# Long convolution and spectral mixing on one NeuronCore: the first tick of a pair moved to PSUM banks 6 and 7, in two parts by channels

## The chip, the cores and the metric

The kernel runs on one core of a Trainium2 chip. The metric is the device time of one execution in microseconds (us). The engines are TensorE (PE in the profile, its weight loads PEld), VectorE (DVE), ScalarE (ACT), GpSimd (POOL) and SyncE (SP); the last two mostly issue DMAs here.

## The reference

The input x has 8 batches of 5696 positions and 128 channels; h has one filter a channel. The first step is a causal convolution along the positions, the second a mixing of the 64 lowest modes with a relu layer behind it:

```python
def _attn_ref(x, h):                      # x: (8, 5696, 128), h: (5696, 128)
    L = 2 * S
    Yf = np.fft.rfft(x, n=L, axis=1) * np.fft.rfft(h, n=L, axis=0)[None]
    return np.fft.irfft(Yf, n=L, axis=1)[:, :S, :]

def _moe_ref(x, w_r, w_i, w_ch):          # x: what _attn_ref gave
    X = np.fft.rfft(x, axis=1)
    Y[:, :64] = X[:, :64] mixed over channels by the complex w_r + i w_i, per mode
    u = x + np.fft.irfft(Y, n=S, axis=1)
    return u + np.maximum(u @ w_ch, 0.0)
```

## The kernel before

The 5696 positions are 89 rows (`NQ`) of 64 columns (`J`). The batches go in four pairs (`NP`, index `g_`; the two batches of a pair are `b` = 0 and 1). The Fourier transform of a pair is done in two steps of matmuls:

1. **First transform, 32 tiles** (`a_tile`, L461). Tile j has four matmuls of 180 columns (input `Xin`, constant `F`) into two PSUM banks, for the channels 4j to 4j+3. VectorE or ScalarE copies the result into `As` in SBUF; tile 31 is copied half by each ("both"). Tiles 6 to 31 of the next pair are made between two pairs, in the loop at L740: this is the *border*. Tile 28 lies in banks 6 and 7, tile 29 in 0 and 1, tile 30 in 2 and 3, tile 31 in 4 and 5. The copies of 28 and 30 are ScalarE's, that of 29 VectorE's.
2. **23 ticks** (`tick`, L649; `NT` = 23, four frequencies of 90 each). Tick t has
   - the *second transform* (`second`, L605): for each of four frequencies and two parts (`r`) a pair of matmuls, one for each batch, on 64 rows of the array each (`As` with the constant `M`, 64x128). The result for batch 0 goes to one bank, that for batch 1 to the next one (`slot_of`, L600). A matmul takes all 128 channels, so it needs the copies of all 32 tiles;
   - the *products* with the filter's spectrum `Hs` on VectorE into `U` (`products`, L616). In most ticks ScalarE first copies both banks to `Xs` (SBUF), and VectorE reads that (L637). In tick 0, VectorE takes batch 0 straight from PSUM, while ScalarE copies batch 1's bank to `Xs`, from which VectorE then takes it (L629). Every fourth tick (t % 4 == 3, pairs 1 to 3) reads PSUM straight for both.
   - two ticks later (`LC`): four matmuls with 512 columns of `U` (constant `Wc`) into one of the banks 4, 5, 6 (`ZBANK`) for each batch, copied by ScalarE to `Zs`, and written to HBM by a DMA on SP's queue;
   - three ticks later (`LM`): matmuls of `Zs` with `G` that add up in bank 7 (`MB`).

In the first pair (`g_` = 0), the ticks up to 16 also make the filter's spectrum (`filter_tick`, L486: matmuls `Ah` with `M` into banks 2 and 3, copied to `Hs` by VectorE), and all second transforms of these ticks use banks 0 and 1. In the later pairs, odd ticks from 1 on do the second transform of the next tick as well (`twin`).

Order of work: every engine runs its instructions in the order in which the program adds them. A recorder (L22) keeps, for each token (a bank, an `As` tile, a `U` buffer), its last writer and readers, and puts semaphore waits ahead of an instruction from them. Matmuls do not wait for matmuls; two VectorE instructions that write the same `U` token do wait for each other. An instruction that waits holds all those behind it on its engine.

At a border the order on TensorE is: tile 31, eight dummy matmuls into banks 6 and 7 (`keep(8, 6)`, L743; they use only the constant `F` and nobody reads them), tick 0's second transform into banks 0 and 1, tick 1's into banks 2 and 3, tick 2's into banks 0 and 1, then tick 0's four `U` matmuls.

After the four pairs comes a last stage (from `mix`, L806): mixing of the modes (`XT` with `W`), the inverse transform (`ZT`, `S4`, `IBs`, `C`) and the relu layer (`WI`), with DMAs of the output.

Of the kernel before, what the change touches and what calls it, by code (L numbers as in the profile page):

```python
# [4 lines left out]
P = 128  # L5
# [118 lines left out]
def bass_long_conv_fft__then__afno_spectral_mix_kernel(nc, x, h, moe_w_r, moe_w_i, moe_w_ch, out):  # L124
    B, S, D = x.shape
# [159 lines left out]
    def ap(t, row, p0, n, off, dims):  # L285
        return bass.AP(t, p0 * row + off, [[row, n]] + [list(d) for d in dims])
# [5 lines left out]
    def pv(bank, off, dims, p0=0, n=P):  # L292
        return bass.AP(ps, p0 * 4096 + bank * 512 + off, [[4096, n]] + [list(d) for d in dims])
# [28 lines left out]
    def mm(o, l, r, st, sp, reads, writes):  # L322
        R.add("tensor", lambda h_: h_.matmul(o, l, r, start=st, stop=sp), reads, writes)  # L323
# [100 lines left out]

    W1, W2, WI = wc_sb[:, 0:P], wc_sb[:, P:2 * P], wi_sb[:, :]
    XSLOT = [0, 2]
    ZBANK = [4, 5, 6]
    MB = 7
    WARM = 92
# [152 lines left out]
    def with_h_at(g_, t):  # L582
        return g_ == 0 and t + LH < NT
# [14 lines left out]
        return g_ > 0 and t % 4 == 3  # L598

    def slot_of(g_, t):  # L600
        if g_ == 0 or t == 0:
            return XSLOT[(t + 1) % 2 if t and not with_h_at(g_, t) else 0]
        return XSLOT[((t - 1) // 4 + t) % 2]

    def second(g_, t):  # L605
        sl = slot_of(g_, t)
        for i, k in enumerate(ticks[t]):
            for r in range(2):
                for b in range(2):
                    col = k * 3 * J + (J if r == 0 else 0) + b * J  # L610
                    mm(pv(sl + b, i * D, [[1, D]]),
                       ap(m_sb, MW, J * b, J, col, [[1, P]]),
                       ap(a_sb, AW, J * b, J, (2 * k + r) * D, [[1, D]]), r == 0, r == 1,
                       AST + mtok(k), [bank(sl + b)])

    def products(g_, t, sl):  # L616
        n = len(ticks[t])
        bk = [bank(sl), bank(sl + 1)]
        i = t % NU
        hv = bass.AP(h_sb, KT * t * D, [[2 * HW, P], [HW, 2], [0, 2], [1, n * D]])  # L620
        uv = bass.AP(u_s[i], 0, [[2048, P], [1024, 2], [512, 2], [1, n * D]])
        src = pv(sl, 0, [[0, 2], [512, 2], [1, n * D]])
        if t == 0:
            e = turns("e", list(range(NXS)))
            evac(bass.AP(x_s[e], 512, [[1024, P], [1, n * D]]), pv(sl + 1, 0, [[1, n * D]]), [bank(sl + 1)], [("xs", e)], eng="scalar")
            hv = bass.AP(h_sb, 0, [[2 * HW, P], [HW, 2], [1, n * D]])
            for b, s_, tok in ((0, pv(sl, 0, [[0, 2], [1, n * D]]), bank(sl)),
                               (1, bass.AP(x_s[e], 512, [[1024, P], [0, 2], [1, n * D]]), ("xs", e))):
                R.add("vector", lambda e, b=b, s_=s_: e.tensor_tensor(bass.AP(u_s[i], b * 512, [[2048, P], [1024, 2], [1, n * D]]), s_, hv, MULT),  # L629
                      [tok, ("h", t, 0), ("h", t, 1, 0), ("h", t, 1, J)], [("u", i)])  # L630
            return
        if not straight(g_, t):
            e = onchip.get((g_, t))
            if e is None:
                e = copied(g_, t, sl)
            src, bk = bass.AP(x_s[e], 0, [[1024, P], [0, 2], [512, 2], [1, n * D]]), [("xs", e)]
        R.add("vector", lambda e: e.tensor_tensor(uv, src, hv, MULT),  # L637
              bk + [("h", t, 0), ("h", t, 1, 0), ("h", t, 1, J)], [("u", i)])
# [10 lines left out]
    def tick(g_, t):  # L649
        if g_ + 1 < NP:  # L650
            for i in range(2 * XC):
                if t == XPLACE[g_ > 0][i]:
                    x_place(i, bass.AP(x_room(g_ + 1, i), 0, [[XB, NQ], [D, XN], [1, D]]), xtok(i))
        with_h = with_h_at(g_, t)
        if t < NT:
            of_two = t > 0 and twin(g_, t - 1)
            if not of_two:
                second(g_, t)
            products(g_, t, slot_of(g_, t))
            if twin(g_, t):  # L660
                second(g_, t + 1)
                if straight(g_, t):
                    copied(g_, t + 1, slot_of(g_, t + 1))
        drain = list(border[t]) if t in border and g_ + 1 < NP else []
        if drain and t >= NT:
            j, sl, e = drain.pop(0)
            a_tile(j, [sl], e)
        if g_ + 1 < NP:
            i = t // 2 - 1 if t % 2 == 0 else -1
            if g_ == 0:  # L670
                i = XLATE.index(t) + NXH if t in XLATE else -1
            if 0 <= i < 2 * XC:
                x_load(g_ + 1, i, x_room(g_ + 1, i), xtok(i), [("u", t % NU)] + AST)
        if LC <= t < NT + LC:
            s_ = t - LC
            n = len(ticks[s_])
            i, zi = s_ % NU, zroom(g_, s_)
            zb = [turns("z", ZBANK) for b in range(2)]
            for b in range(2):
                for r in range(2):  # L680
                    mm(pv(zb[b], 0, [[1, n * D]]), (W1, W2)[r], u_s[i][:, r * 1024 + b * 512:r * 1024 + b * 512 + n * D],
                       r == 0, r == 1, [("u", i), ("wc",)], [bank(zb[b])])
                evac(bass.AP(z_s[zi], b * D, [[1024, P], [2 * D, n], [1, D]]),
                     pv(zb[b], 0, [[D, n], [1, D]]), [bank(zb[b])], [("zs", zi, b)], eng="scalar",
                     after=once(("zx", zi, b), Z_OLD) if zi >= NZ else ())
            zo = (g_ * NK + KT * s_) * P * 256
            dma("sync", bass.AP(zs, zo, [[256, P], [P * 256, n], [1, 256]]),
                bass.AP(z_s[zi], 0, [[1024, P], [256, n], [1, 256]]), "z",
                [("zs", zi, 0), ("zs", zi, 1)], [("zd", g_, s_)])
            if drain and t >= NT:  # L690
                j, sl, e = drain.pop(0)
                a_tile(j, [sl], e)
        if LM <= t < NT + LM:
            s_ = t - LM
            zi = zroom(g_, s_)
            for i, k in sorted(enumerate(ticks[s_]), key=lambda q: (s_ > 0 or q[1] != 1, q)):
                for b in range(2):
                    if k % 2:
                        o, off, n, sl = pv(MB, b * P, [[1, P]]), (k + 1) // 2 * P, P, (k + 1) // 2
                    else:  # L700
                        ms, off = even[k]
                        n, sl = 2 * len(ms), 0
                        dims = [[M, 2]] if len(ms) == 1 else [[ms[1] - ms[0], 2], [M, 2]]
                        o = pv(MB, b * P + ms[0], dims)
                    mm(o, z_s[zi][:, i * 256 + b * P:i * 256 + b * P + P], g_sb[:, off:off + n],
                       k == 1 and b == 0, k == NK - 1 and b == 1, [("g", sl // GP), ("zs", zi, b)], [bank(MB)])
        if drain and t < NT + LM - 1:
            j, sl, e = drain.pop(0)
            a_tile(j, [sl], e)
        if with_h:  # L710
            filter_tick(t + LH, [2, 3])
# [11 lines left out]
    for g_ in range(NP):  # L723
        if g_ == NP - 1:
            load_w(0)
            load_w(1)
        for t in range(NT + LM):
            tick(g_, t)
            if g_ == 0 and t < 2:
                keep(8, 4)  # L730
            assert g_ + 1 < NP or not wp
            if g_ == NP - 1 and t in early:
                pace[:] = [("u", min(t, NT - 1) % NU)]
                early[t]()
        evac(bass.AP(xt, 2 * g_ * XTW + M, [[B * XTW, P], [XTW, 2], [1, P]]), pv(MB, 0, [[P, 2], [1, P]]),
             [bank(MB)], [("xt", g_)], 1.0 / 64, eng="scalar", after=[("ag", k) for k in range(NS + 2 * XN, NK)])
        evac(bass.AP(xt, 2 * g_ * XTW, [[B * XTW, P], [XTW, 2], [1, M]]), pv(MB, M, [[P, 2], [1, M]]),
             [bank(MB)], [("xtn", g_)], -1.0 / 64, eng="vector" if g_ + 1 == NP else "scalar", after=[("ag", k) for k in range(NS + 2 * XN, NK)])
        if g_ + 1 < NP:
            for j in range(6, 32):  # L740
                a_tile(j, [(4, 6, 0, 2)[(j - 7) % 4] if j > 6 else 0], "both" if j == 31 else (A, V)[(j - 6) % 9 % 2])
                if j == 31:
                    keep(8, 6)  # L743
                if wp and j % 2 == 1:
                    dst, src_, ring, tok = wp.pop(0)
                    dma("gpsimd", dst, src_, ring, (), [tok], after=[("as", j)])
# [192 lines left out]
```

## Time and profile before

| what | us |
|---|---|
| median of 3 runs | 382.4 (381.59 to 383.15) |
| the profiled execution | 381.7 |
| its span, first to last instruction | 379.9 |
| TensorE busy | 359.7 |
| ScalarE busy | 314.4 |
| VectorE busy | 294.9 |
| GpSimd busy | 75.1 |

The mean clock granted to TensorE was 0.989 of full speed. The three borders lie at about 90 to 107, 146 to 162 and 201 to 217 us of the span; the last stage begins at about 258 us.

How to read the profile: a row of the timeline has the start and length in us, the engine, the line of the program, the operation, the output and input by name and shape, how many instructions were merged into the row, and in brackets how long the engine stood idle before and what ended that. The chain of waits is the sequence of work and waits that ended last, followed back from the last instruction; each piece has its start and length. A group row has busy time and the mean length of one in ns. Matmuls overlap: one of 128 columns shows 0.22 us, though the next pair starts 0.06 us later.

### The profile page before, as it was taken

To read this page: it belongs to the slowest core of one execution; us is meant where nothing else is said; L and a number is where in the kernel's file an instruction comes from. 1 tells how busy PE (TensorE), PEld (TensorE's weight loads), DVE (VectorE), ACT (ScalarE), POOL (GpSimd) and SP (SyncE) were. 2 spreads that over 40 slices of the span, in tenths; PEclk is the share of its full clock that TensorE was granted. 3 is DMA by queue.
4 is the path that set the end of the run, shared out by engine and by line. 5 is a ranking of instruction groups with operands and counts; after the bars stand their busy time and mean duration, and the time that the engine had idled before them with its cause. 6 is when DMAs were issued, how large, how long until landed. Compare 5 with 4: busy or idle time off the path is not lost.

```text
span 379.9 us, 12434 instructions
## 1 busy us (share of the span) xinstructions
PE 359.7 (95%) x5346; PEld 278.9 (73%) x5346; DVE 294.9 (78%) x333; ACT 314.4 (83%) x495; POOL 75.1 (20%) x117
## 2 busy tenths in 40 slices
PE   7889899999989999989999999999999999999994
PEld 7778766666856666856667856668889889988873
DVE  3649799878988999989998888882437767766666
ACT  8469689898989997989997999995457776788884
POOL 8713012100642220733310301124000000000000
PEclk9999999999999999999999999998899999999999
DMA  7999959979799997999995989999999999999878
GB/s 149 206 292 362 248 147 231 236 205 267 87 143 202 238 250 217 103 125 212 259 253 168 95 302 364 372 360 383 372 390 376 374 412 404 418 405 382 319 296 320
DMA packets 87048, 103.94 MB, mean 274 GB/s; under 512 B 22730, under 2 KB 72522, under 8 KB 83438
## 3 DMA queue, kind: packets, MB, share of 16 engines
q1 hardware_dynamic: 64610, 81.33, 60.7%
q0 software_dynamic: 22384, 21.83, 34.8%
q8 instruction: 42, 0.69, 0.7%
q14 instruction: 12, 0.10, 0.1%
HBM read 70.61 MB, written 51.12 MB: 320 GB/s over the span
## 4 chain that ended last, share of the span: by engine, by line
PE 66%; ACT 13%; DVE 7%; DMA 6%; issue 4%; POOL 3%; DVEq 0%; ACTq 0%; POOLq 0%
PE ps L323 65%; ACT As L313 7%; DMA Xr<-in_x_dram 4%; DVE As L317 2%; ACT Zs L311 2%; DMA zscr<-Zs 2%; DVE U L629 2%; ACT Zt L311 2%; POOL Xr L320 2%; ACT Xs L311 1%; DVE Xin L365 1%; ACT R L871 1%; POOL Hin L320 1%; DVE U L637 1%; DVE Hs L315 1%
## 5 line engine op out<-in xcount | busy, mean ns | idle before, releaser
L637 DVE TENSOR_TENSOR U<-Xs,Hs 128x2048 f16<-128x2048 f16 (+1 forms) x73 | 86.9, 1192 | 14.3 <-ACT Xs L311 11.3
L323 PE MATMUL ps<-U,Wc 128*128 128x512 f16 (+1 forms) x368 | 94.2, 376 | 0.5 <-DVE U L629 0.5
L311 ACT CAST Xs<-ps 128x1024 f16<-128x1024 f32 (+1 forms) x77 | 75.0, 978 | 12.3 <-PE ps L323 7.3
L311 ACT CAST Zs<-ps 128x512 f16<-128x512 f32 (+1 forms) x132 | 69.2, 594 | 2.0 <-PE ps L323 1.7
L872 DVE TENSOR_TENSOR O<-ps,R 128x512 f32<-128x512 f32 x81 | 52.3, 684 | 20.1 <-ACT R L871 11.2
L317 DVE TENSOR_SCALAR As<-ps 128x720 f16<-128x720 f32 (+1 forms) x67 | 55.6, 880 | 5.7 <-PE ps L323 4.0
L871 ACT ACTIVATE R<-ps 128x512 f32<-128x512 f32 (+1 forms) x92 | 50.5, 591 | 8.5 <-PE ps L323 8.4
L323 PE MATMUL ps<-F,Xin 128*128 128x180 f16 x512 | 52.4, 250 | 3.7 <-DVE Xin L365 2.2
L323 PE MATMUL ps<-As,M 64*128 64x128 f16 x1440 | 50.3, 217 | 3.8 <-DVE U L629 3.0
L323 PEld LDWEIGHTS ps<-F,Xin 128*128 128x128 f16 x512 | 44.5, 155 | 11.1 <-DVE As L317 3.2
L313 ACT ACTIVATE As<-ps 128x720 f16<-128x720 f32 (+1 forms) x65 | 45.8, 768 | 7.2 <-PE ps L323 6.6
L323 PE MATMUL ps<-WI,UT 128*128 128x256 f16 x360 | 51.1, 278 | 0.5 <-ACT UT L311 0.4
L311 ACT CAST UT<-ps 128x712 f16<-128x712 f32 x46 | 34.5, 752 | 19.2 <-PE ps L323 18.0
L323 PEld LDWEIGHTS ps<-U,Wc 128*128 128x128 f16 x368 | 28.6, 97 | 29.7 <-ACT Zs L311 3.8
L323 PEld LDWEIGHTS ps<-As,M 64*128 64x128 f16 x1440 | 40.5, 94 | 10.0 <-DVE U L629 3.7
L323 PEld LDWEIGHTS ps<-WI,UT 128*128 128x128 f16 x360 | 39.0, 152 | 3.4 <-issue 1.8
L323 PE MATMUL ps<-IBs,C 128*128 128x356 f16 x128 | 40.3, 325 | 0.1
L320 POOL DMA_DIRECT2D Xt<-in_x_dram x40 | 21.5, 541 | 81.2 <-PE ps L323 80.7
L323 PEld LDWEIGHTS ps<-G,Zs 128*128 128x128 f16 x512 | 26.1, 96 | 14.5 <-ACT Zs L311 2.0
L637 DVE TENSOR_TENSOR U<-ps,Hs 128x2048 f16<-128x2048 f32 x15 | 34.3, 2284 | 0.0
L323 PE MATMUL ps<-G,Zs 128*128 128x128 f16 (+2 forms) x512 | 32.2, 192 | 0.1
L311 ACT CAST Zt<-ps 128x512 f16<-128x512 f32 x52 | 28.5, 622 | 0.2 <-PE ps L323 0.2
(74 smaller groups left out, 489.0 us busy)
## 6 DMA issues: line engine op xcount, KB each, us to landing
out_dram<-O SPq DMA_DIRECT2D x39, 512.0 KB, 6.9
zscr<-Zs SPq DMA_DIRECT2D x62, 256.0 KB, 6.8
zscr<-Zt SPq DMA_DIRECT2D x26, 256.0 KB, 6.7
Xt<-in_x_dram POOLq DMA_DIRECT2D x20, 320.0 KB, 7.3
W<-wscr SPq DMA_DIRECT2D x4, 1024.0 KB, 7.0
ZT0a<-zscr SPq DMA_DIRECT2D x4, 1024.0 KB, 8.2
M<-cM POOLq DMA_DIRECT2D x5, 720.0 KB, 17.0
ZT1a<-zscr SPq DMA_DIRECT2D x3, 1024.0 KB, 8.3
```

Source lines behind the costliest of these rows:

```text
L311: R.add(e, lambda h_: h_.copy(dst, src), reads, writes, after=after)
L313: R.add(e, lambda h_: h_.activation(dst, src, COPY, scale=scale), reads, writes, after=after)
L315: R.add(e, lambda h_: h_.tensor_copy(dst, src), reads, writes, after=after)
L317: R.add(e, lambda h_: h_.tensor_scalar_mul(dst, src, scale), reads, writes, after=after)
L320: R.add(eng, lambda h_: h_.dma_start(dst, src), reads, writes, ring=ring, after=after)
L323: R.add("tensor", lambda h_: h_.matmul(o, l, r, start=st, stop=sp), reads, writes)
L365: R.add("vector", lambda e: e.tensor_copy(bass.AP(x_sb, i * XN * XS, [[XW, NQ], [XS, XN], [1, D]]), src), list(toks) + XZ, [("xin", i)])
L629: R.add("vector", lambda e, b=b, s_=s_: e.tensor_tensor(bass.AP(u_s[i], b * 512, [[2048, P], [1024, 2], [1, n * D]]), s_, hv, MULT), [tok, ...
L637: R.add("vector", lambda e: e.tensor_tensor(uv, src, hv, MULT), bk + [("h", t, 0), ("h", t, 1, 0), ("h", t, 1, J)], [("u", i)])
L871: R.add("scalar", lambda e: e.activation(rv, src_r, RELU), bk, [("r", i % NR)], after=once(("r", i % NR), G_ALL + XTT + [("y", 0), ("y", 1 ...
L872: R.add("vector", lambda e: e.tensor_tensor(ov, src_u, rv, ADD), bk + [("r", i % NR)], [key + (h_,)], after=once(key, old))
```

## The change

Tick 0's second transform uses banks 6 and 7 (`ZSLOT`) in every pair. For the pairs 1 to 3 it is cut by channels (`DA` = 116): the channels 0 to 115, which come from the tiles 0 to 28, take the place of the dummies, behind tile 31's matmuls, and wait for the copies of the tiles 0 to 28 only. In tick 0, batch 0's product for these channels is taken from PSUM; then come the last 12 channels of batch 1 (bank 7), ScalarE's copy of bank 7 and batch 1's product. The last 12 channels of batch 0 (bank 6) come in tick 1, behind tick 1's second transform, with a third, small product.

```diff
+    ZSLOT, DA = 6, 116
     def slot_of(g_, t):
-        if g_ == 0 or t == 0:
-            return XSLOT[(t + 1) % 2 if t and not with_h_at(g_, t) else 0]
+        if t == 0:
+            return ZSLOT
+        if g_ == 0:
+            return XSLOT[(t + 1) % 2 if not with_h_at(g_, t) else 0]
         return XSLOT[((t - 1) // 4 + t) % 2]
-    def second(g_, t):
+    def second(g_, t, d0=0, d1=D, bs=(0, 1)):
         sl = slot_of(g_, t)
+        rd = AST if d1 == D else [("as", j) for j in range(d1 // 4)]
         for i, k in enumerate(ticks[t]):
             for r in range(2):
-                for b in range(2):
+                for b in bs:
...
-                    mm(pv(sl + b, i * D, [[1, D]]),
+                    mm(pv(sl + b, i * D + d0, [[1, d1 - d0]]),
...
+    def first_u(b, s_, row, tok, d0, d1):
+        n = len(ticks[0])
+        R.add("vector", lambda e: e.tensor_tensor(
+            bass.AP(u_s[0], b * 512 + d0, [[2048, P], [1024, 2], [D, n], [1, d1 - d0]]),
+            bass.AP(s_[0], s_[1] + d0, [[row, P], [0, 2], [D, n], [1, d1 - d0]]),
+            bass.AP(h_sb, d0, [[2 * HW, P], [HW, 2], [D, n], [1, d1 - d0]]), MULT),
+              [tok, ("h", 0, 0), ("h", 0, 1, 0), ("h", 0, 1, J)], [("u", 0)])
     def products(g_, t, sl):
...
+            if g_ == 0:
+                copy_b()
+                first_u(0, (ps, sl * 512), 4096, bank(sl), 0, D)
+                first_u(1, (x_s[e], 512), 1024, ("xs", e), 0, D)
+                return
+            first_u(0, (ps, sl * 512), 4096, bank(sl), 0, DA)
+            second(g_, 0, DA, D, (1,))
+            copy_b()
+            first_u(1, (x_s[e], 512), 1024, ("xs", e), 0, D)
             return
...
             if not of_two:
-                second(g_, t)
+                if g_ == 0 or t:
+                    second(g_, t)
+                if g_ and t == 1:
+                    second(g_, 0, DA, D, (0,))
+                    first_u(0, (ps, slot_of(g_, 0) * 512), 4096, bank(slot_of(g_, 0)), DA, D)
             products(g_, t, slot_of(g_, t))
...
                 if j == 31:
-                    keep(8, 6)
+                    second(g_ + 1, 0, 0, DA)
```

More of the change, by code (lines that the diff above doesn't have):

```diff
@@ L600, in slot_of @@
     def slot_of(g_, t):
-        if g_ == 0 or t == 0:
-            return XSLOT[(t + 1) % 2 if t and not with_h_at(g_, t) else 0]
+        if t == 0:
+            return ZSLOT
+        if g_ == 0:
+            return XSLOT[(t + 1) % 2 if not with_h_at(g_, t) else 0]
         return XSLOT[((t - 1) // 4 + t) % 2]
-    def second(g_, t):
+    def second(g_, t, d0=0, d1=D, bs=(0, 1)):
         sl = slot_of(g_, t)
+        rd = AST if d1 == D else [("as", j) for j in range(d1 // 4)]
         for i, k in enumerate(ticks[t]):
             for r in range(2):
-                for b in range(2):
+                for b in bs:
                     col = k * 3 * J + (J if r == 0 else 0) + b * J
-                    mm(pv(sl + b, i * D, [[1, D]]),
+                    mm(pv(sl + b, i * D + d0, [[1, d1 - d0]]),
                        ap(m_sb, MW, J * b, J, col, [[1, P]]),
-                       ap(a_sb, AW, J * b, J, (2 * k + r) * D, [[1, D]]), r == 0, r == 1,
-                       AST + mtok(k), [bank(sl + b)])
+                       ap(a_sb, AW, J * b, J, (2 * k + r) * D + d0, [[1, d1 - d0]]), r == 0, r == 1,
+                       rd + mtok(k), [bank(sl + b)])
+    def first_u(b, s_, row, tok, d0, d1):
[5 more added lines that the diff above has]
+              [tok, ("h", 0, 0), ("h", 0, 1, 0), ("h", 0, 1, J)], [("u", 0)])
     def products(g_, t, sl):
@@ L624, in products, with copy_b @@
             e = turns("e", list(range(NXS)))
[L625 to L630, printed above, removed]
+            def copy_b():
+                evac(bass.AP(x_s[e], 512, [[1024, P], [1, n * D]]), pv(sl + 1, 0, [[1, n * D]]), [bank(sl + 1)], [("xs", e)], eng="scalar")
+            if g_ == 0:
[7 more added lines that the diff above has]
+            first_u(1, (x_s[e], 512), 1024, ("xs", e), 0, D)
             return
```

## The prediction

> **What bounds the kernel now.** I read the page first, then the chain of waits in order of time, then the timeline around one border between two pairs.
>
> ```profile
> span 379.9 us, 12434 instructions
> PE 66%; ACT 13%; DVE 7%; DMA 6%; issue 4%; POOL 3%; DVEq 0%; ACTq 0%; POOLq 0%
> ```
>
> Two thirds of the chain is TensorE. So a change counts where TensorE stands still on the chain, and the chain in order of time (start, length, what) shows such a place at each border:
>
> ```profile
> 106.70 0.67 PE ps L323 x16
> ...
> 109.43 27.27 PE ps L323 x430
> ...
> 161.86 0.67 PE ps L323 x16
> ...
> 162.53 1.23 DVE U L629
> ...
> 163.85 0.70 DVE U L629
> ...
> 164.59 27.27 PE ps L323 x430
> ...
> 217.01 0.67 PE ps L323 x16
> ...
> 219.75 33.33 PE ps L323 x524
> ```
>
> The three borders are alike: 16 matmuls (the second transform of tick 0), two VectorE products one behind the other, and then an unbroken TensorE stretch of 27 to 33 us. From the start of the 16 to that stretch is 109.43 - 106.70 = 2.73 us, 164.59 - 161.86 = 2.73 us and 219.75 - 217.01 = 2.74 us. The unbroken stretch is what I take as proof that time won ahead of it is kept: behind it everything hangs on TensorE. The timeline of the middle border (start, length, engine, what, idle before):
>
> ```profile
> 160.80 0.79 PE L323 MATMUL ps<-F 128*128 128x180 f16 x8
> 161.86 1.07 PE L323 MATMUL ps<-As,M 64*128 64x128 f16 x32 [0.27 <-ACT As L313]
> 162.55 1.50 ACT L311 CAST Xs<-ps 128x512 f16<-128x512 f32 x2 [0.74 <-PE ps L323]
> 163.80 0.62 PE L323 MATMUL ps<-As,M 64*128 64x128 f16 x16 [0.87 <-DVE U L629]
> 164.45 2.44 DVE L637 TENSOR_TENSOR U<-Xs,Hs 128x2048 f16<-128x2048 f16 x2
> 164.63 1.01 ACT L311 CAST Xs<-ps 128x1024 f16<-128x1024 f32 x1 [0.58 <-DVE U L629]
> ```
>
> Row one is the eight dummies. Row two is tick 0 and tick 1 together (2 x 16). Row four is tick 2: it waited 0.87 us because tick 0's first product still read banks 0 and 1. The last row waited 0.58 us for the second product, which frees its Xs buffer. Single copies, from narrower windows:
>
> ```profile
> 159.94 0.80 ACT L313 ACTIVATE As<-ps 128x720 f16<-128x720 f32 x1
> 161.08 0.54 DVE L317 TENSOR_SCALAR As<-ps 128x360 f16<-128x360 f32 x1
> 161.30 0.51 ACT L313 ACTIVATE As<-ps 128x360 f16<-128x360 f32 x1
> 162.55 0.59 ACT L311 CAST Xs<-ps 128x512 f16<-128x512 f32 x1 [0.74 <-PE ps L323]
> ```
>
> The first is tile 28, done at 160.74; the next two are the halves of tile 31, done at 161.62 (VectorE) and 161.81 (ScalarE). Tick 0 starts 0.05 us after the latter.
>
> **The change, part by part.** Durations by shape, and TensorE with weights that change at every matmul:
>
> ```profile
> L629 DVE TENSOR_TENSOR U<-ps,Hs 128x1024 f16<-128x1024 f32 x4 | 4.9, 1225 | 3.9 <-PE ps L323 3.9
> L629 DVE TENSOR_TENSOR U<-Xs,Hs 128x1024 f16<-128x1024 f16 x4 | 2.8, 692 | 0.4
> L637 DVE TENSOR_TENSOR U<-ps,Hs 128x2048 f16<-128x2048 f32 x15 | 34.3, 2284 | 0.0
> L317 DVE TENSOR_SCALAR XT<-ps 128x128 f16<-128x128 f32 x1 | 0.3, 291 | 2.6 <-ACT XT L313 2.6
> 259.34 1.02 PEld L323 LDWEIGHTS ps<-XT,W 128*128 128x128 f16 x32 [0.32 <-issue]
> 259.37 1.11 PE L323 MATMUL ps<-XT,W 128*128 128x16 f16 x32 [0.20 <-issue]
> ```
>
> A product out of PSUM costs (2284 - 1225)/1024 = 1.034 ns an element and 1225 - 1024 x 1.034 = 166 ns fixed. So the 116-channel product (2 x 4 x 116 = 928 elements) is 1.13 us and the 12-channel one (96) is 0.27 us, in line with 0.29 for the 128 elements of the XT copy. The new access patterns split a run of 512 into four; I take that as free.
>
> *Dummies out, 116 channels in.* The eight dummies (0.79 us) go; 16 matmuls take their place behind the same release, tile 28's copy. Row two above gives (1.07 - 0.22)/15 = 0.057 us a pair (0.22 is one matmul's own length), so 7 x 0.057 + 0.22 = 0.62: 160.80 to 161.42. This lies under the copies of tiles 29 to 31 and is free. VectorE ends its half of tile 31 at 161.62 and begins the product at once: 161.62 + 1.13 = 162.75, against 162.53 + 1.23 = 163.76 now.
>
> *Tail, bank 7.* It waits for tile 31 as tick 0 does now, so 161.86. Eight matmuls, all on the same half of the rows, 12 columns each. This shape is not in the trace. The nearest is the 16-column matmul on the whole array, whose weights change each time: (1.02 - 0.10)/31 = 0.03 us each, where 0.10 is a single load. The upper end is a pair's 0.057, the lower end nothing. I take 0.03: 7 x 0.03 + 0.19 (one short matmul's length) = 0.40 instead of 0.62. Now the Xs copy starts 162.55 - 161.86 - 0.62 = 0.07 behind the last result; so 161.86 + 0.40 + 0.07 = 162.33, done 162.92.
>
> *Second product* (bank 7's, from Xs): it waits for that copy, and for the first product (0.09 us from end to start now, 163.76 to 163.85): 162.92 + 0.04 = 162.96, plus 0.69 = 163.65.
>
> *Tail, bank 6.* TensorE runs tick 1 first (161.86 + 8 x 0.03 = 162.10 to 162.56), then waits for the first product to leave bank 6 (162.75 + 0.05). Behind that wait stand tick 2's transform and everything else of TensorE; the tail is done at 162.80 + 0.40 = 163.20, still ahead of 163.65, so not on the path. Its product is: 163.65 + 0.09 + 0.27 = 164.01. The first matmul on U follows 0.05 later: **164.06 instead of 164.59, 0.53 us a border**.
>
> *What is late next.* Tick 2's transform goes to banks 0 and 1, which tile 29 left long ago: 163.04 instead of 163.80. The Xs copy behind it waits for the second product, 163.74 instead of 164.63. VectorE reaches tick 1's product at 164.0 instead of 164.45. All three move by 0.45 us or more, so TensorE's stretch starts 0.53 earlier with its feeders no later against it. No DMA is issued by the moved steps; the loads of tick 2 on the GpSimd queue wait for tick 2's product and move with it.
>
> *Group 0.* Tick 0 goes to banks 6 and 7 there too, so tick 1 no longer waits for bank 0.
>
> ```profile
> 45.12 0.62 PE L323 MATMUL ps<-As,M 64*128 64x128 f16 x16 [0.35 <-DVE U L629]
> 46.52 0.41 PE L323 MATMUL ps<-Ah,M 64*128 64x64 f16 x16 [0.77 <-DVE Hs L315]
> 47.58 0.62 PE L323 MATMUL ps<-As,M 64*128 64x128 f16 x16
> 49.29 1.23 DVE L637 TENSOR_TENSOR U<-Xs,Hs 128x2048 f16<-128x2048 f16 x1 [0.64 <-ACT Xs L311]
> ```
>
> Tick 1 (row one) wins its 0.35 us and more, but the filter step behind it (row two) waits for VectorE's copy Hs out of the shared banks 2 and 3, which stands behind the two products as before; tick 2 and the product at 49.29 follow from there. I count nothing.
>
> **Sum:** 3 x 0.53 = 1.6 us. The profiled execution took 381.7 us (span 379.9): 380.1. Against the median of 382.4 that is **380.8 us**, 0.42% less.
>
> Ends of the unknowns per border: with 0.057 for the tail matmuls the copy is 0.19 later, and a 12-channel product at 0.29 adds 0.02: gain 0.32. With tails at nothing, the first product decides: 162.75 + 0.09 + 0.69 + 0.09 + 0.27 + 0.05 = 163.94, gain 0.65. Times three: 1.0 to 2.0.
>
> **Rivals.**
>
> *No gain: the tails cost what they save.* If a weight load on one half of the rows can't run beside the matmul ahead, each tail matmul costs its 0.10 load more, 0.13 apart. A tail is then 7 x 0.13 + 0.19 = 1.10: the Xs copy is done at 163.62, the second product at 164.35; tick 1 runs to 163.36, bank 6's tail to 164.46, its product to 164.77, and TensorE goes on at 164.82, 0.23 late: 382.4 + 0.7 = 383.1. The same sum breaks even at 0.11 apart. Against it: 0.03 on the whole array, where all rows are shared. The other road to nothing is that the gain is absorbed behind the border, should ScalarE and not TensorE set the pace there (382.4); the chain has TensorE for 27 us unbroken. Together 0.12.
>
> [...]
>
> *Slower: the clock.* TensorE's granted clock fell once in mid-run. Three stretches of 3.41 us (busy time of TensorE first, the clock third from the end), and what TensorE ran in the second and in the first:
>
> ```profile
> 43.82:47.23 3.41, 2.28 (x61) 1.79 (x54) 2.92 (x4) 1.60 (x2) 0.00 (x0) 1.00 0.96 255
> 258.86:262.27 3.41, 3.21 (x97) 3.08 (x93) 2.07 (x2) 3.06 (x3) 1.45 (x1) 1.00 1.04 387
> 262.27:265.69 3.42, 3.19 (x75) 3.02 (x73) 0.69 (x1) 0.25 (x2) 0.00 (x0) 0.50 1.10 381
> ```
>
> ```profile
> L323 PE MATMUL ps<-XT,W 128*128 128x16 f16 x73 | 2.7, 192 | 0.2 <-issue 0.2
> L323 PE MATMUL ps<-S4b,ZT0b 84*128 84x89 f16 x12 | 1.4, 204 | 0.0
> L323 PE MATMUL ps<-S4a,ZT0a 128*128 128x89 f16 x12 | 1.4, 204 | 0.0
> ```
>
> ```profile
> L323 PE MATMUL ps<-F 128*128 128x180 f16 x13 | 1.4, 243 | 0.0
> L323 PE MATMUL ps<-Ah,M 64*128 64x64 f16 x32 | 0.8, 190 | 0.8 <-DVE Hs L315 0.8
> L323 PE MATMUL ps<-As,M 64*128 64x128 f16 x16 | 0.6, 217 | 0.4 <-DVE U L629 0.4
> ```
>
> Ahead of the fall TensorE took 73 x 16 + 24 x 89 = 3304 columns; 13 x 180 + (32 x 64 + 16 x 128)/2 = 4388 (pairs run side by side) kept the clock. After the change the emptiest 3.41 us of a border (160.65 to 164.06) hold one or two matmuls of tile 31 (260), 8 x 116, two transforms (2 x 8 x 128) and the tails (16 x 12): 3430. Now they are 161.2 to 164.61 with three dummies and three transforms (3 x 180 + 3 x 8 x 128): 3610. If the level lies between these two, and the border falls into a stretch just so, half a clock for 3.41 us costs up to 1.7 us a border against 0.53 won: 3 x 1.2 = 3.5, 385.9. The two are close together, so the chance is small: 0.09.
>
> [...] The fall here came after TensorE was busy for 3.21 of 3.41 us, so the trace says few columns, not idleness.
>
> **How the numbers follow.** About 0.5% (1.9 us) is what a measurement of this kernel can tell from no change. Forecast, 1.0 to 1.9 us won: 0.52. More than 1.9 (tails nearly free, or a median that scatters as the shown runs do, 381.59 to 383.15): 0.27. No gain: 0.12, of which 0.02 for tails so long that it is over 1.9 us late. Clock: 0.09. So faster 0.27; same 0.52 + 0.10 = 0.62; slower 0.09 + 0.02 = 0.11. Range 379.6 to 382.8: the sum's ends (382.4 - 2.0 = 380.4 and 381.4), widened by the 0.8 by which a run stands off the median, and up over most of the no-gain case; it leaves out the clock.
>
> **What would show it.** At each border: the 116-channel product at 161.6 less 161.86, that is 0.2 us ahead of the tail; tails of 0.4 us; the stretch of U matmuls 2.2 us after the tail's start instead of 2.73; no 0.87 us wait of tick 2. Wrong if the tail's matmuls stand 0.06 us or more apart, if the U stretch is broken by ScalarE, or if a 0.50 clock shows near a border.

## The result, and the profile after

The changed kernel takes 379.9 us (median of 14 runs, 378.84 to 381.0), the kernel before 381.56 us (14 runs, 379.92 to 383.15). The ratio is 0.9952, 95% interval 0.9934 to 0.997: by that ratio 1.8 us (1.1 to 2.5) were won; the two medians alone differ by 1.7. Forecast were 380.8 us and 1.6 us less. In a second set of runs the same kernel gave 379.78 us and 0.9953 (0.9934 to 0.9972).

The chain of waits of the changed kernel, the three borders in order of time (start, length, what):

```profile
105.73 0.36 PE ps L323 x8
...
107.85 27.26 PE ps L323 x430
...
160.28 0.37 PE ps L323 x8
...
160.68 0.59 ACT Xs L311
...
161.29 0.70 DVE U L622
...
162.09 0.27 DVE U L622
...
162.40 27.26 PE ps L323 x430
...
214.84 0.37 PE ps L323 x8
...
216.96 33.33 PE ps L323 x524
```

Eight tail matmuls, the Xs copy, the second product, the third product, then the unbroken stretch. From the first tail matmul to the stretch it is 107.85 - 105.73 = 2.12, 162.40 - 160.28 = 2.12 and 216.96 - 214.84 = 2.12 us, where it was 2.73, 2.73 and 2.74: 0.61 to 0.62 a border, 1.84 in all. What follows kept its length: the stretches are 27.26, 27.26 and 33.33 us against 27.27, 27.27 and 33.33, and from a stretch to the next border's tail it is 160.28 - 107.85 = 52.43 us, against 161.86 - 109.43 = 52.43. So in these two executions nothing of the gain is given back inside a pair.

Single executions differ there. A second profile of the changed kernel has the same borders, 2.12, 2.12 and 2.11 us, but 53.19 and 52.68 us from a stretch to the next border's tail. The first 400 matmuls of a stretch take 25.77 us in every profile of this case but one, in which the clock fell; the differences come behind them, towards the end of a pair. That the gain holds in spite of them is read from the run times, not from one profile.

The timeline of the middle border (start, length, engine, what, idle before):

```profile
159.30 0.58 PE L323 MATMUL ps<-As,M 64*128 64x116 f16 x16
159.94 1.11 DVE L622 TENSOR_TENSOR U<-ps,Hs 128x928 f16<-128x928 f32 x1
...
160.28 1.65 PE L323 MATMUL ps<-As,M 64*128 64x12 f16 x48 [0.40 <-ACT As L313]
160.68 2.43 ACT L311 CAST Xs<-ps 128x512 f16<-128x512 f32 x3 [0.45 <-PE ps L323]
161.11 0.65 PEld L323 LDWEIGHTS ps<-As,M 64*128 64x128 f16 x24 [0.18 <-DVE U L622]
161.29 0.69 DVE L622 TENSOR_TENSOR U<-Xs,Hs 128x1024 f16<-128x1024 f16 x1 [0.23 <-ACT Xs L311]
162.09 0.26 DVE L622 TENSOR_TENSOR U<-ps,Hs 128x96 f16<-128x96 f32 x1
162.26 2.35 DVE L655 TENSOR_TENSOR U<-Xs,Hs 128x2048 f16<-128x2048 f16 x2
...
162.40 1.04 PE L323 MATMUL ps<-U,Wc 128*128 128x512 f16 x4 [0.47 <-DVE U L622]
```

The first product now begins 0.34 us *before* the tail, where it began 0.66 us behind the start of tick 0's transform (162.52 against 161.86). It ends at 161.05, and VectorE waits 0.23 us for the Xs copy: batch 1's road, not batch 0's, now sets the path. The weight loads of TensorE wait 0.18 us for bank 6 (the row at 161.11), and tick 2's wait of 0.87 us is gone.

The profiled execution shows more than the borders give: its span is 377.0 us against 379.9, 2.9 less. Of that, 0.97 us lies ahead of the first border (105.73 against 106.70). The chain of the kernel before has a stall there for which the profile shows no wait, in the middle of 16 matmuls:

```profile
66.00 2.41 PE ps L323 x56
68.41 0.63 issue
69.05 1.01 PE ps L323 x22
```

The changed kernel's chain has one unbroken piece in these 4 us. The same stall, 0.87 us at 68.50, stands in the first experiment below, which has the changed kernel's banks in the first pair; the second profile of the changed kernel has it too, 0.53 us at 69.97, and the second experiment, with the first pair as before, has not. So it belongs to single executions and not to the change. It is a part of the scatter of 2 to 3 us among the runs of one kernel; what releases TensorE there, the profile does not show, and the rest of the 0.97 us was not followed up.

### The profile page after: what moved, and what is told of

It is laid out like the page before. It is cut to its first block, busy times and chain, and to the rows that moved or that the text cites. A ratio compares the mean times of both kernels' runs of the same rounds, so it can differ in the third digit from the quotient of the medians.

```text
span 377.0 us, 12488 instructions
## 1 busy us (share of the span) xinstructions
PE 359.5 (95%) x5370; PEld 279.1 (74%) x5370; DVE 294.8 (78%) x336; ACT 314.1 (83%) x495; POOL 75.0 (20%) x117
## 4 chain that ended last, share of the span: by engine, by line
PE 72%; ACT 10%; DMA 6%; DVE 5%; POOL 3%; issue 3%; DVEq 0%; POOLq 0%
PE ps L323 72%; ACT As L313 7%; DMA Xr<-in_x_dram 4%; DVE As L317 2%; DMA Xt<-in_x_dram 2%; POOL Xr L320 2%; DVE U L622 1%; ACT Zs L311 1%; ACT Xs L311 1%; POOL Hin L320 1%; DVE Xin L365 1%; DVE Hs L315 1%; ACT R L893 1%; ACT Zt L311 1%; DVE U L655 0%
## 5 line engine op out<-in xcount | busy, mean ns | idle before, releaser
L323 PE MATMUL ps<-As,M 64*128 64x128 f16 (+2 forms) x1488 | 51.9, 215 | 1.2 <-ACT As L313 1.2
L323 PEld LDWEIGHTS ps<-U,Wc 128*128 128x128 f16 x368 | 28.7, 97 | 30.3 <-ACT Zs L311 3.7
L323 PEld LDWEIGHTS ps<-As,M 64*128 64x128 f16 x1488 | 41.6, 94 | 7.5 <-ACT As L313 1.7
```

## The experiments

The theory: the gain is the first product's earlier start, made possible by the split by channels; the path is then tail, Xs copy, second product, third product. Rivals: it is the free bank for tick 2; it is the first pair; it is the dummies; and, for an improvement, that another engine sets the pace behind the border. Ratios are to the kernel before, run beside them.

**Banks alone.** Tick 0 in banks 6 and 7, undivided; dummies and order of the products as before.

```diff
-                    second(g_ + 1, 0, 0, DA)
+                    keep(8, 6)
...
-            if g_ == 0:
+            if True:
                 copy_b()
...
-                if g_ == 0 or t:
-                    second(g_, t)
-                if g_ and t == 1:
-                    second(g_, 0, DA, D, (0,))
-                    first_u(0, (ps, slot_of(g_, 0) * 512), 4096, bank(slot_of(g_, 0)), DA, D)
+                second(g_, t)
```

> Tick 0 in banks 6 and 7 in every pair, but whole, behind tile 31's copies, with the eight dummies as before. Theory (the gain is the earlier start of the first product, through the split by channels): tick 2's transform no longer waits 0.87 us, but the U matmuls still start 2.7 us after tick 0, since the two products are as late as before; time within 0.1 us a border of before, 0 to -0.3 us in all. Rival (the gain is the free bank, which lets tick 2 go ahead): the U matmuls start 0.5 us earlier a border and most of the 1.8 us is there.

Measured: 381.86 us, ratio 0.9993 (0.9967 to 1.0019). Its timeline at the middle border:

```profile
161.85 1.51 PE L323 MATMUL ps<-As,M 64*128 64x128 f16 x48 [0.27 <-ACT As L313]
162.50 1.23 DVE L622 TENSOR_TENSOR U<-ps,Hs 128x1024 f16<-128x1024 f32 x1 [0.90 <-PE ps L323]
...
163.83 0.69 DVE L622 TENSOR_TENSOR U<-Xs,Hs 128x1024 f16<-128x1024 f16 x1
...
164.58 0.61 PE L323 MATMUL ps<-U,Wc 128*128 128x512 f16 x2 [1.22 <-DVE U L622]
```

All 48 matmuls of three ticks run in one piece; tick 2 waits for nothing. And the U matmuls still come 2.73 us behind tick 0. The wait of 0.87 us has only moved, into one of 1.22 us ahead of the U matmuls. The theory held; the wait with the largest number on TensorE was not the one that ended last.

**Pairs only.** The changed kernel, with the first pair's tick 0 back in banks 0 and 1.

```diff
         if t == 0:
-            return ZSLOT
+            return ZSLOT if g_ else XSLOT[0]
```

> The changed kernel, with tick 0 of the first pair back in banks 0 and 1; the other pairs as changed. Theory: the first pair's new banks are worth nothing, so the time is that of the changed kernel, 1.8 us below before (within 0.3), and the first border lies where a stall of fetching or of a DMA in the first pair puts it, not 1 us later by rule. Rival: the first pair gave the 1 us by which the changed profile reached its first border earlier; then this one is only 0.8 us below before.

Measured: 379.75 us, 0.9935 (0.9913 to 0.9956), as fast as the changed kernel within the intervals: 2.5 us below before by this ratio, where 1.8 was expected and 0.8 would have been the rival's. The tail of its first border starts at 105.94 us, where the kernel before has 106.70 and the changed one 105.73. The first pair's new banks are worth nothing that can be measured. Whether fetching or a DMA is behind the stall in the first pair, as the theory supposes, no profile here shows.

**Dummies back.** Six dummies behind the 116-channel matmuls.

```diff
                     second(g_ + 1, 0, 0, DA)
+                    keep(6, 0)
```

> The changed kernel with six dummies put back, behind the 116-channel matmuls, into banks 0 and 1. Theory: TensorE stands still there anyway (0.4 us ahead of the tail), so the time is that of the changed kernel within 0.3 us, and the clock of the borders is 1.00 in both. Rival (part of the gain is the dummies' removal, or the dummies guard the clock): slower by up to 0.4 us a border, or faster where a border's clock fell without them.

Measured: 379.2 us, 0.9941 (0.9917 to 0.9964): the gain is there with dummies too. In its trace the copy of tile 31 ends at 162.09 and the U matmuls start at 164.34, 2.25 us later, against 162.40 - 160.23 = 2.17: the dummies reach into the tail and cost 0.08 us a border, 0.24 in all, which the 0.3 us of the expectation allows. The clock was whole at all borders, as expected; it fell at 28.7 us, in the first pair, and in the last stage, as in every profile (at 262.27 us in the kernel before, at 260.32 in the changed one).

**Batch 1 first.** Each batch of tick 0's U matmuls waits for its own products, and batch 1 comes first.

```diff
-              [tok, ("h", 0, 0), ("h", 0, 1, 0), ("h", 0, 1, J)], [("u", 0)])
+              [tok, ("h", 0, 0), ("h", 0, 1, 0), ("h", 0, 1, J)], [("ub", b)], after=[("u", 0)])
...
-            for b in range(2):
+            for b in ((1, 0) if g_ and s_ == 0 else (0, 1)):
...
-                       r == 0, r == 1, [("u", i), ("wc",)], [bank(zb[b])])
+                       r == 0, r == 1, [("u", i), ("wc",)] + ([("ub", b)] if s_ == 0 else []), [bank(zb[b])])
```

> The changed kernel with one change of order: tick 0's U matmuls take batch 1 first in the pairs 1 to 3, and each batch waits for its own products only, so the small third product (0.26 us and 0.1 us of waiting for the second) leaves the path. Theory (the path is tail, Xs copy, second product, third product): the U matmuls start 0.37 us earlier a border, 1.75 instead of 2.12 us behind the tail, and the time is 1.1 us below the changed kernel, 2.9 below before. Rival (behind the border another engine sets the pace by now): no more than 0.3 us below the changed kernel.

Measured: 378.42 us, 0.9914 (0.988 to 0.9948). Its chain, first and second border:

```profile
106.49 0.37 PE ps L323 x8
...
107.50 0.87 DVE U L622 x2
...
108.41 27.27 PE ps L323 x430
...
161.01 0.37 PE ps L323 x8
...
162.02 0.70 DVE U L622
...
162.77 27.27 PE ps L323 x430
```

At the second border the third product is off the chain, and from the tail to the stretch it is 1.76 us instead of 2.12: 0.36 won, as expected. At the first one it is 1.92, and two products stand on the chain: batch 1's U matmuls get bank 6 there, which the third product still reads. This was overlooked in the edit; the next one takes care of it.

**Batch 1 first, banks exchanged.** On top of the edit above:

```diff
             zb = [turns("z", ZBANK) for b in range(2)]
+            if g_ and s_ == 0 and zb[1] == ZSLOT:
+                zb.reverse()
```

> As batch 1 first, but the two U banks of that tick are exchanged at the border where batch 1 would get bank 6, which the small third product still reads (there the U matmuls had come only 0.19 us earlier, at the other two 0.36). Theory: all three borders now have the U matmuls 1.81 us behind the end of tile 31's ScalarE copy, against 2.17 in the changed kernel and 2.79 before; 1.1 us below the changed kernel, 2.9 below before. Rival (the time won here is lost again at the end of the pair, where the last load of the next input lands): the stretch from the first U matmul to the last of a pair grows by as much in each pair, and the time is that of the changed kernel.

> Batch 1 first with the banks exchanged, unaltered, once more. Theory: 2.9 us below before (3 x 0.98), ratio 0.992; rival (the gain over the changed kernel was scatter): 0.995.

Measured: 379.12 us, 0.9924 (0.9897 to 0.995), and again 378.24 us, 0.9906 (0.9879 to 0.9932). This is the best version; the second interval lies wholly below that of the changed kernel, the first overlaps it. The two traces have the tail-to-stretch distance at 1.75 to 1.76 us at all borders. The rival asks for the end of the pairs; that of the third pair (between the second and the third border) in the first of the two:

```profile
189.50 0.47 issue
...
189.99 7.83 DMA Xt<-in_x_dram
...
197.84 0.70 DVE Xin L365
```

and in the second one:

```profile
190.16 7.27 DMA Xt<-in_x_dram
...
197.46 0.70 DVE Xin L365
```

The chain no longer runs through ScalarE there (as in the kernel before) but through the last load of the next pair's input, 7.83 or 7.27 us to land. From stretch to next tail the third pair takes 214.69 - 161.56 = 53.13 and 214.29 - 161.73 = 52.56 us, where it is 214.84 - 162.40 = 52.44 in the changed kernel; the second pair takes 52.45 in both, against 52.43. But the shorter border isn't what puts the load there. In "banks alone", whose border is as long as before, the chain of the third pair runs through the same load, and the pair takes 217.46 - 164.58 = 52.88 us:

```profile
193.02 7.58 DMA Xt<-in_x_dram
```

So some tenths of a us of a pair (0.46 here, up to 0.71 above) can hang on when one load lands, with the long border as with the short one. What the rival asks for, each pair longer by as much as its border is shorter (0.98 us), is not there.

**The changed kernel again**, beside the others.

> The changed kernel unaltered, beside the others on the same chip: 1.86 us below before by the three borders (3 x 0.62), whatever one profile's scatter in the first pair or in the last stage shows.

Measured: 379.78 us, 0.9953 (0.9934 to 0.9972): 1.8 us, as the three borders say. The profiled execution took 383.08 us: its clock fell at 28.6 us, where TensorE had waited for the first input (busy for 1.51 us of 3.41 in 25.09 to 28.50, a clock of 0.51 in the 3.42 behind), and its second and third pairs were longer (above). Its borders are as short as in the first profile.

**Split at 64, split at 120.** `ZSLOT, DA = 6, 64` and `6, 120`.

> The changed kernel with the split at channel 64 instead of 116, so the first product has 512 elements, the third 512 too. Theory (the third product stands on the path, the first does not): the first product ends 0.43 us earlier and gains nothing, the third takes 0.70 instead of 0.26 us, the U matmuls come 2.6 us behind tile 31's copy: 0.15 to 0.2 us a border left of the gain, 0.5 in all below before. Rival (it is enough to start the first product early, whatever is left for later): same time as the changed kernel or faster.

> The split at channel 120, so the first part waits for tile 29's copy on VectorE, about 0.35 us later. Theory: the first product then ends 0.33 us later, behind the Xs copy, and becomes the one that the second product waits for (0.2 us late); the third is 0.03 shorter: the U matmuls 2.3 us behind tile 31's copy, 0.15 us a border worse than the split at 116. Rival (the third product's length alone decides): 0.03 us a border better.

Measured: 381.91 us, 1.0001 (0.998 to 1.0022), and 380.84 us, 0.9979 (0.9961 to 0.9996). At 64 the path is as expected: tail at 106.33, stretch at 108.93, 2.60 us, so 3 x 0.13 of the gain are left, which the interval allows; the first product's early end bought nothing. At 120 the U matmuls come 164.12 - 161.67 = 2.45 us behind tile 31's copy, expected 2.3: its timeline

```profile
159.80 1.87 ACT L313 ACTIVATE As<-ps 128x720 f16<-128x720 f32 x3
...
161.78 1.16 DVE L622 TENSOR_TENSOR U<-ps,Hs 128x960 f16<-128x960 f32 x1 [0.30 <-PE ps L323]
162.12 1.50 ACT L311 CAST Xs<-ps 128x512 f16<-128x512 f32 x2 [0.44 <-PE ps L323]
...
163.04 0.69 DVE L622 TENSOR_TENSOR U<-Xs,Hs 128x1024 f16<-128x1024 f16 x1
```

has the first product ending at 162.94, behind the Xs copy (162.12 + 0.59 = 162.71), and the second waits for it. Both splits bear out which product decides; measured from the end of tile 31's copy, the first product ended 1.27 - 0.82 = 0.45 us later than with the split at 116, where I had taken 0.33.

In the profiled execution of the split at 64 the clock fell at a border. Four stretches of 3.41 us (TensorE's busy time first, its clock third from the end):

```profile
157.06:160.48 3.42, 3.42 (x42) 2.95 (x42) 3.29 (x5) 3.42 (x6) 2.42 (x4) 1.00 1.39 135
160.48:163.89 3.41, 1.75 (x64) 1.46 (x63) 2.58 (x6) 2.91 (x5) 2.67 (x4) 1.00 1.60 155
163.89:167.30 3.41, 3.29 (x32) 1.91 (x34) 2.72 (x4) 1.56 (x3) 0.52 (x2) 0.52 1.01 100
167.30:170.71 3.41, 3.41 (x52) 2.06 (x50) 3.04 (x2) 2.97 (x5) 0.56 (x2) 0.98 0.89 154
```

TensorE was busy for 1.75 of 3.41 us, and half a clock followed for one such stretch. (The clock changed at 164.04 and 167.45 us, so these four stretches are cut 0.15 us early and show 0.52 and 0.98; in 160.62 to 164.04, TensorE was busy for 1.64.) What it cost is read from the unbroken stretch behind:

```profile
108.93 27.27 PE ps L323 x430
...
164.01 28.88 PE ps L323 x422
...
194.06 7.54 DMA Xt<-in_x_dram
```

The first 400 matmuls behind this border took 27.38 us instead of 25.77: 1.61 us. From this stretch to the next tail it took 218.46 - 164.01 = 54.45 us instead of 161.41 - 108.93 = 52.48; the other 0.4 us is the last load, which stands on the chain here as in "banks alone". So the rival of the clock, which I had priced at up to 1.7 us a border, is real, in a kernel whose borders are emptier.

**Split at 64 with six dummies**, to see whether filling the border holds the clock.

> The split at channel 64 with six dummies put behind the first part (banks 0 and 1), where TensorE stands still. In the split at 64 alone the clock fell at a border of the profiled execution and 5 of 12 runs had a mean clock under 0.9865, against 5 of 59 of before. Theory (a border with few columns for TensorE lets the clock fall): with 6 x 180 = 1080 columns more no clock falls at a border, at most 2 of 12 runs are under 0.9865, and the median is 0.5 us below before (3 x 0.13), where the split at 64 alone was level with it. Rival (the falls had another cause or were chance): the same share of low clocks as without the dummies.

Measured: 381.14 us, 0.9987 (0.9967 to 1.0008), 0.5 us below before as expected, though the interval takes in no change; and 3 of 12 runs under 0.9865 where I had asked for 2 at most. Its profile has no fall at a border, but one at 28.0 us, behind TensorE's wait for the first input. Without traces of the other runs it can't be told where theirs fell: the run times don't settle whether the dummies hold the clock (the last section has a count of columns that speaks for it). Dummies don't do away with low clocks as a whole: "dummies back" had 3 of 12 runs under 0.9865, and its profile has a fall at 28.7 us. In the changed kernel itself no profile shows a fall at a border, and 3 of 27 runs were under 0.9865, against 6 of 76 of the kernel before, those run beside the experiments.

## Why the prediction was right, step by step

*The bound and what is kept.* The prediction took the unbroken TensorE stretch behind a border as proof that time won ahead of it stays. It does for the stretch itself, 27.26 us against 27.27, while the border went from 2.73 to 2.12. Behind the stretch, at the end of a pair, the chain leaves TensorE; there both profiles have 52.43 us from stretch to tail, but other executions up to 0.8 us more (53.19 and 52.68 in the second profile of the changed kernel).

*Dummies out, 116 channels in.* 0.62 us forecast, 0.58 measured, hidden under the copies as said. The product took 1.11 us (forecast 1.13) and started 0.09 us before VectorE's last copy ended (159.94 against 159.50 + 0.53 = 160.03). No wait stands between these two; the next pair without one, the third product and tick 1's, overlaps by the same 0.09 (162.26 against 162.09 + 0.26 = 162.35). The product was 0.1 us earlier ahead of the tail than forecast, which changed nothing, since the Xs copy ended later:

```profile
159.50 0.53 DVE L317 TENSOR_SCALAR As<-ps 128x360 f16<-128x360 f32 x1
...
159.30 0.58 PE L323 MATMUL ps<-As,M 64*128 64x116 f16 x16
159.94 1.11 DVE L622 TENSOR_TENSOR U<-ps,Hs 128x928 f16<-128x928 f32 x1
160.28 0.11 PEld L323 LDWEIGHTS ps<-As,M 64*128 64x128 f16 x2 [0.56 <-ACT As L313]
160.28 0.18 PE L323 MATMUL ps<-As,M 64*128 64x12 f16 x1 [0.40 <-ACT As L313]
```

*Tail.* 0.40 us forecast, 0.37 measured; with 0.18 for one, (0.37 - 0.18)/7 = 0.027 us apart, where I took 0.030 from the XT rows. So eight matmuls in a row on one half of the rows stood 0.027 us apart here, with a load of 0.09 us each (two of them show 0.11 in the row above), and not the 0.13 of the rival of tails that cost what they save: it is out.

*Copy and products.* The Xs copy started 0.40 us behind the tail's start, forecast 0.47: the tail was 0.03 shorter, and of the 0.07 us that I had added behind the last result 0.03 were left. These two make 0.07 of the 0.08 us between forecast and measured, 2.20 and 2.12. Second product 0.70 (0.69), wait 0.10 (0.09), third product 0.27 (0.27), 0.04 to TensorE (0.05).

*What is late next.* Tick 1's product came no later than forecast (162.26, so 1.98 us behind the tail's start, forecast 2.14), and TensorE's wait for bank 6 cost nothing on the path. Not foreseen: the last load of the next pair's input can stand on the chain at the end of a pair. It does so with the long border too ("banks alone").

*Group 0.* Nothing, as said: the pairs-only experiment is as fast.

*Sum.* 1.6 us forecast, 1.84 by the trace, 1.8 measured. The absolute 380.8 was 0.9 too high because it set out from a median of three runs, 382.4; over 14 runs the same kernel has 381.56. The rival that the gain is absorbed is out by the run times, 1.8 us in both sets, and by the stretches behind the borders. The clock rival did not come to pass at the borders. Its level, an estimate from two stretches of one trace, was put too high: of the 3304 columns ahead of the fall, 12 x 89 were on 84 of 128 rows and counted whole. Counted by rows, the clock fell in these traces behind 2387 to 3054 columns in 3.41 us and stayed behind 3139 and more (last section), and the emptiest 3.41 us of a border has 3535 to 3571 in the changed kernel. By this count the rival had no room at these borders.

## What to carry to other kernels

Ask of a wait not how long it is but whether the work behind it is what ends last: the longest wait on TensorE at this border (0.87 us, a busy bank) was worth nothing, and cutting the first product, so that it left the path, was worth 0.6 us. Where a step waits for the last of many tiles, cut it along the axis by which the tiles arrive, so that all but the last tiles' share is done early; then look whether what is left (here a product of 96 elements, 0.36 us with its wait) must stand ahead of everyone, or only ahead of its own user.

## What the runs showed of the hardware

At the border of the split at 64 the granted clock fell behind 3.41 us in which TensorE's longest wait was 1.17 us, ahead of the U matmuls, and 1.64 us were busy; in the last stage of the kernel before it fell behind 3.41 us whose longest wait was 0.20 us (258.86 to 262.27). The stretches at half clock are 3.41 us (164.04 to 167.45 in the split at 64) or twice that (262.27 to 269.10 in the kernel before, 260.32 to 267.14 in the changed one).

Busy time doesn't tell the two kinds apart: behind 1.68 us (24.80 to 28.21, the changed kernel) the clock stayed, behind 3.21 (258.86 to 262.27, the kernel before) and 3.42 (256.90 to 260.32, the changed kernel) it fell. A count of columns does in these traces. Cut each of the twelve into stretches of 3.41 us from a fall of its clock, from 6 us of the span to the end of TensorE's work, and count the columns of the matmuls that it records, each by the share of the array's 128 rows that it uses, and by parts (0.057 us for 128 columns) where it lies across a cut. Behind 16 of the stretches at full clock the clock fell; they have 2387 to 3054 columns (2593 in 258.86 to 262.27 of the kernel before, 2651 in 256.90 to 260.32 of the changed kernel). Behind all the others it stayed; the emptiest has 3139 (in the kernel before it has 3947, 43.82 to 47.23, in the first profile of the changed kernel 3318, 24.80 to 28.21). Behind the last matmul the clock fell too, after 3.42 us without one (374.91 to 378.33, the kernel before). What the chip goes by, the traces do not show. At a border the emptiest 3.41 us, wherever the cut lies, has 3634 to 3650 columns in the kernel before, 3535 to 3571 in the changed kernel, 2417 to 2713 in the split at 64, and 3709 to 3750 in the same with six dummies. By this count no border of the changed kernel comes down to the stretches behind which the clock fell; those of the split at 64 do where the cut lies so, and with six dummies none does.

Profiles of one kernel differ by a stall of TensorE for which they show no wait (none and 0.53 us in the first pair of the changed kernel, at a place where the kernel before has 0.63 and "banks alone" 0.87), by the landing of one load (7.27 and 7.83 us in the best version), and by where the clock falls (at 28.6 us in the second profile of the changed kernel, nowhere ahead of the last stage in the first); single profiles are not to be compared by their span here, but border by border.
